# Another hand-written order for a windowed-attention and GELU-MLP kernel on one core

## Chip, cores, metric

The kernel runs on one core of a Trainium2 chip. The metric is the device time of one execution in microseconds (us). Its engines are TensorE (PE, weight loads shown as PEld), VectorE (DVE), ScalarE (ACT), GpSimd (POOL) and SyncE (SP). Each engine works through its own instructions in the order in which the program gives them; engines wait for one another, and for DMAs, on semaphores.

## What is computed

The reference is attention with a sliding window of 128 keys and 4 sink keys, followed by a two-layer MLP with a sigmoid-approximated GELU:

```python
scores = (q @ k.T) / sqrt(64)                 # q, k, v: (4 batches, 8 heads, 768, 64)
keep   = (pos_k < 4) | ((pos_q - pos_k >= 0) & (pos_q - pos_k < 128))
a      = softmax(where(keep, scores, -1e9))
x      = (a @ v) as (3072 tokens, 512)
h      = x @ w_in                             # (512, 2048)
out    = (h * sigmoid(1.702 * h)) @ w_out     # (2048, 512), float32 out
```

## The kernel before

**Tiles.** The 3072 tokens are 24 blocks of 128 (block b is row block b % 6 of batch b // 6). The first block of each batch (0, 6, 12, 18) goes first, then the others. Two blocks make a group g for the MLP.

**One block.** Its q and k come by a DMA that POOL issues and that casts them to fp16 (`qkn`, L315). They are transposed by PE (`tq`, L408, the first 8 blocks) or by a transposing DMA that SP issues (L429). PE makes the scores against the own and the previous key block (`own`, `prv`, L488; the first four blocks use L463 and a mask by matmul, L455). DVE merges the two under the window's mask (L531), takes maxima (L543, L562) and subtracts them (L600). ACT takes exp (L633; L586 for a half of the first four blocks). The result `a` is transposed, by PE for the first four blocks (`ta`, L696) and from then on by a DMA that SP issues (`at<-a`, L734). POOL cuts it into the own and the previous part by two selects (L645, L639). PE multiplies with the values (`av`, L755 for the sink keys, L761, L765), DVE normalizes (L776, L777), and PE (`tx`, L790) or a DMA transposes the result into `xT`.

**The sink keys' values.** The first four value rows of a batch come by a small SP DMA into `vsa` (L358). `vsa` is set to one beforehand by a DVE memset (L271). A product with a mask then builds `vsb` (L363), which every `av` of that batch with a previous block needs (L755).

**One group's MLP.** `hT` (L825) has 8 pieces of 32 matmuls (group 0: 16 matmuls of half the width each), ACT takes the GELU (L855), `o` (L876) has for each block four pieces of 4 matmuls with `gT`, a copy to `osb` by ACT or DVE and an SP store (L894). `w_in` and `w_out` are loaded in four quarters each by POOL (L324, L333). Piece f of `hT` needs its quarter of `w_in`; piece n of `o` needs quarter n of `w_out`.

**The order.** Nothing is scheduled by the compiler. A planner object only lists 918 operations, numbered 0 to 917 as they are added. `ORDER` (L58) is a string of tokens such as `104V`: emit operation 104 on DVE (P PE, A ACT, V DVE, G POOL, S SP). Walking through it sets the order on all five engines. `FILL` (L100) puts dummy matmuls (L905) ahead of some PE operations. `HOME` (L107) moves PSUM tiles from the ring they belong to (`mm` 3 banks, `own` 2, `pv` 2) to another one.

Operations that the change and the prediction speak of:

| number | what |
|---|---|
| 15 | DVE memset of `vsa` (L271) |
| 100 | SP load of `vsa`, batch 0 (L358) |
| 104 | building `vsb`, batch 0 (L363) |
| 49, 50 | POOL loads of q and k of block 4 (L315) |
| 35, 33 | POOL loads of `w_in`, quarters 3 and 1 (L324) |
| 38, 39, 42, 43 | POOL loads of `w_out`, quarters 0, 1, 2, 3 (L333) |
| 44, 45 | POOL loads of v, blocks 1 and 2 (L306) |
| 590, 582 | the first two pieces of `hT`, group 0 |
| 592, 593 | first two pieces of `o` of block 0; they need `w_out` quarters 0 and 1 |
| 598, 626 | first pieces of `o` of two other blocks |
| 234, 211 | SP transposes `at<-a` of blocks 2 and 1 |
| 235, 212 | POOL selects of blocks 2 and 1 |
| 236, 213 | `av` of blocks 2 and 1, first half |

POOL's loads use eight semaphores in turn, so that a load is issued only when the load eight places ahead of it has landed.

Of the kernel before, what the change touches and what calls it, by code (L numbers as in the profile page):

```python
# [55 lines left out]


ORDER = """  # L58
9V 4V 0S 17V 2V 15V 5G 13V 1S 22G 11V 19V 101S 18V 12V 7S 23G 6S 8S 28G 29G 20A 21A 3G 27G 108P 110P 109A 10V 113P
26G 16V 14V 130P 111V 114P 24G 32G 116V 131A 112A 132P 36G 133V 118A 115V 174P 37G 135P 117V 136P 175A 176P 138V  # L60
119A 154P 177V 25G 140A 120P 121A 137V 179P 31G 139V 180P 155A 152P 182V 35G 153V 141A 181V 33G 157P 184A 183V 142P
158P 34G 159V 122P 144P 185A 143A 40G 196P 123V 161V 126P 41G 145A 186P 160V 146P 198P 163A 148P 30G 127V 124P 187A
125V 46G 162A 188P 147V 164P 53G 149V 199A 166P 165V 150P 167V 189A 190P 168P 151V 128P 192P 169V 170P 129A 590P
171V 193V 582P 591A 197V 191V 172P 201P 47G 50G 586P 173A 194P 578P 583A 195V 587A 200P 579A 608P 49G 202V 610P 38G
55G 204V 203V 611A 609A 219P 221P 205V 588P 206V 589A 134A 580P 209V 208V 614P 39G 581A 105G 207V 222V 584P 42G 220V
576P 43G 585A 615A 612P 56G 577A 52G 613A 223P 604P 156A 225V 44G 226V 606P 45G 227V 616P 228V 224P 617A 607A 229V
232V 605A 230V 242P 618P 244P 231V 243V 592P 245V 626P 619A 210A 247P 246P 593P 249V 251V 248V 265P 267P 627P 250V
233A 620P 252V 266V 234S 254V 628P 268A 253V 621P 100S 255V 256A 211S 269P 622P 271V 257S 272V 594P 274V 288S 273V
629P 623P 624A 235G 270P 595P 630A 275V 104V 598P 596A 212G 599P 597S 276V 278V 631S 236P 277V 279A 238P 237V 600P
239V 59G 280S 213P 215P 51G 48G 214V 240P 601P 216V 241A 217P 602A 289P 61G 218V 290P 291V 642P 58G 292V 634P 71G  # L70
643A 294V 646P 293V 57G 295V 632P 68G 296V 647A 635A 297V 636P 62G 633A 306P 258G 640P 308V 309V 638P 641A 298V 310V
67G 73G 644P 311V 639A 637A 65G 648P 645A 654P 299A 64G 259P 655P 281G 307P 649P 312V 300S 313V 656P 314V 54G 261P
324S 315V 284P 260V 316A 650P 285V 262V 282P 657P 283V 301G 317S 178A 263P 286P 264V 651P 287V 603S 360S 664P 69G
652V 658A 662P 66G 665A 674P 60G 672P 70G 663A 675A 666P 78G 673A 325P 318G 660P 328V 327V 326P 304P 661A 667A 329V
668P 63G 330V 676P 669A 331V 74G 305V 670P 332V 302P 333V 671A 321P 303V 677P 322V 319P 682P 320V 334V 323S 342P
335A 344V 653S 345V 683P 678P 347V 343P 684P 346V 336S 348V 679P 350V 625S 351V 685P 349V 659S 352A 378P 692P 381V
686A 337G 353S 680V 379P 693A 696P 697A 380V 396S 690P 382V 80G 691A 383V 384V 688P 386V 76G 694P 385V 689A 102S
354G 387V 361P 695A 698P 364V 363V 700P 77G 699A 366V 340P 79G 701A 365V 338P 362P 388A 710P 339V 341V 355P 367V
711P 370V 368V 357P 356V 704P 389S 369V 702P 358V 371A 359S 414P 703A 705P 416V 372S 418V 712P 390G 417V 415P 706P
432S 419V 420V 713P 422V 83G 421V 707P 397P 82G 373G 708V 724P 400V 709S 399V 722P 423V 401V 714A 725A 393P 398P  # L80
402V 723A 391P 726P 392V 403V 394V 81G 716P 727A 85G 72G 718P 405V 404V 728P 719A 75G 374P 729A 717A 720P 86G 375V
106G 376P 721A 732P 406V 377V 424A 733P 395S 450P 738P 452V 407A 454V 451P 739P 453V 408S 730P 455V 456V 734P 457V
731A 715S 425S 458V 740P 433P 681S 746P 409G 436V 468S 435V 741P 747A 438V 735P 459V 742A 437V 92G 103S 758P 91G
434P 748P 759A 439V 426G 442V 736V 752P 749A 440V 756P 441V 753A 88G 744P 757A 95G 750P 745A 89G 412P 410P 413V 754P
107G 411V 429P 97G 755A 427P 430V 760P 751A 428V 443A 766P 431S 486P 767P 488V 460A 489V 444S 761P 490V 487P 762P
491V 461S 492V 768P 493V 743S 763P 494V 504S 445G 784P 764A 469P 785A 769P 472V 737S 462G 474V 495V 471V 782P 473V
772P 783A 470P 475V 87G 778P 773A 770V 98G 780P 446P 781A 84G 774P 447V 465P 775A 776P 466V 477V 779A 448P 777A 463P
476V 786P 464V 794P 449V 787A 478V 496A 467S 522P 788P 524V 525V 523P 789P 527V 479A 497S 795P 526V 528V 790P 530V
765S 529V 796P 480S 531V 532A 802P 94G 540S 498G 797P 803A 505P 798A 791P 507V 533S 96G 509V 800P 792A 481G 804P
499P 805A 810P 500V 90G 508V 814P 811A 510V 93G 501P 815A 506P 808P 511V 99G 801A 513V 484P 502V 812P 534G 482P 813A  # L90
806P 483V 809A 485V 822P 807A 514V 512V 503S 816P 515A 558P 687S 817P 793S 560V 559P 818P 562V 516S 823P 561V 563V
564V 819P 565V 567V 824P 566V 820V 568A 830P 517G 825P 831A 541P 834P 543V 826A 542P 535P 835A 827S 842P 536V 771S
544V 832P 569S 546V 833A 545V 821S 843A 547V 828P 799S 548V 836P 837A 550V 520P 829A 838P 521V 570G 549V 518P 839A
850P 551A 537P 538V 519V 844P 539S 851P 840P 552S 852P 841A 845P 573P 846P 574V 853P 553G 847P 854A 868P 855S 848A
856P 849S 869A 870P 857A 858P 871A 866P 862P 867A 859A 556P 554P 863A 557V 864P 571P 865A 860P 572V 555V 878P 861A
575S 872P 879P 873P 880P 874P 881P 886P 882V 875P 883S 887A 888P 876A 884P 877S 889A 894P 885A 890P 895A 896P 891A
892P 897A 898P 893A 906P 899A 900P 901P 907P 902P 912P 908P 903P 913P 904V 909P 914P 905S 910A 915P 911S 916A 917S
""".split()

FILL = dict(  # L100
    map(int, x.split(":"))
    for x in """
108:18 130:2 132:1 174:3 154:2 157:8 126:6 188:2 164:1 166:3
""".split()
)

HOME = dict(x.split(":") for x in "0:pv 2:mm 5:own 7:own 8:mm 9:own 10:pv 12:pv 16:own 18:mm 19:pv 21:pv 22:mm 25:own 26:pv 27:mm 28:mm 29:pv 31:pv 32:own 35:pv 37:mm 40:own 41:pv 42:mm 43:mm 44:mm 46:mm 49:pv 50:pv 51:mm 52:own 53:own 54:own 55:pv 56:own 57:pv 59:mm 61:mm 62:own 63:own 64:own 65:pv 67:own 69:own 169:own 173:own 174:own 175:pv 180:pv 181:own 183:pv 185:own 189:pv 194:pv 197:pv 199:own 200:pv".split())  # L107

# [57 lines left out]
def kernel(  # L168
# [728 lines left out]

    for n, ring in HOME.items():
        plan.bufs[int(n)].ring = ring
# [42 lines left out]
```

## Time and profile before

| | |
|---|---|
| median of 3 runs | 227.68 us (227.68 to 227.69) |
| the profiled execution, its own time | 228.61 us |
| its span in the trace | 226.9 us |
| PE busy | 218.1 us, 96% of the span |
| DVE / ACT / POOL busy | 138.7 / 127.0 / 115.3 us |
| mean granted TensorE clock | 1.0 |
| POOL's load queue (q0) | 77,024 packets, 13.37 MB |
| SP's and ACT's DMAs (q1 and q10) | 54,944 packets, 19.1 MB |

The page's "busy" of PE counts overlapping, pipelined matmuls, so that it hides short waits. What a stretch of PE costs is read from the starts of its instructions. In this execution a piece of `hT` follows the next PE operation by 0.87 us, a piece of `o` by 0.86 us, a block's scores by 0.55 us, half an `av` by 0.35 us and a group of four transposes by 0.22 us. These intervals are used for "PE work" below.

### The profile page before, as it was taken

To read this page: it belongs to the slowest core of one execution; us is meant where nothing else is said; L and a number is where in the kernel's file an instruction comes from. 1 tells how busy PE (TensorE), PEld (TensorE's weight loads), DVE (VectorE), ACT (ScalarE), POOL (GpSimd) and SP (SyncE) were. 2 spreads that over 40 slices of the span, in tenths; PEclk is the share of its full clock that TensorE was granted. 3 is DMA by queue.
4 is the path that set the end of the run, shared out by engine and by line. 5 is a ranking of instruction groups with operands and counts; after the bars stand their busy time and mean duration, and the time that the engine had idled before them with its cause. 6 is when DMAs were issued, how large, how long until landed. Compare 5 with 4: busy or idle time off the path is not lost.

```text
span 226.9 us, 5434 instructions
## 1 busy us (share of the span) xinstructions
PE 218.1 (96%) x2238; PEld 153.7 (68%) x2238; DVE 138.7 (61%) x332; ACT 127.0 (56%) x197; POOL 115.3 (51%) x127
## 2 busy tenths in 40 slices
PE   7889999999998999999999999999999999999994
PEld 4668997445774875775685685695695685775862
DVE  5799648876948288888976666668467582031001
ACT  3788675543663744767259347456656666540721
POOL 8995583029996970671980891570790321300000
PEclk9999999999999999999999999999999999999999
DMA  9999999999999999899997999998998175202202
GB/s 127 155 166 205 181 179 200 181 178 236 145 104 148 191 152 165 217 158 125 176 164 107 243 101 121 195 136 101 219 136 181 27 237 97 97 0 49 92 0 92
DMA packets 131992, 32.82 MB, mean 145 GB/s; under 512 B 124640, under 2 KB 129024, under 8 KB 131968
## 3 DMA queue, kind: packets, MB, share of 16 engines
q0 software_dynamic: 77024, 13.37, 78.1%
q1 hardware_dynamic: 53904, 18.85, 40.9%
q10 hardware_dynamic: 1040, 0.26, 0.5%
q8 instruction: 17, 0.28, 0.5%
q14 instruction: 7, 0.06, 0.1%
HBM read 27.36 MB, written 6.29 MB: 148 GB/s over the span
## 4 chain that ended last, share of the span: by engine, by line
PE 85%; DVE 7%; POOL 3%; ACT 2%; issue 1%; POOLq 0%; DVEq 0%
PE hT L825 35%; PE o L876 35%; PE own L488 3%; PE av L761 2%; PE av L765 2%; PE prv L488 2%; PE av L755 2%; DVE mx L562 2%; DVE mx L543 1%; POOL qkn L315 1%; PE tq L408 1%; DVE e L600 1%; POOL at L639 1%; ACT a L586 1%; PE tx L790 1%
## 5 line engine op out<-in xcount | busy, mean ns | idle before, releaser
L825 PE MATMUL hT<-xT,w_in 128*128 128x256 f16 (+1 forms) x832 | 91.9, 264 | 0.3 <-DVE osb L284 0.3
L876 PE MATMUL o<-w_out,gT 128*128 128x512 f16 (+1 forms) x400 | 90.5, 371 | 0.0
L855 ACT ACTIVATE gT<-hT 128x512 f16<-128x512 f32 x96 | 54.9, 597 | 49.9 <-PE hT L825 49.1
L825 PEld LDWEIGHTS <-w_in 128*128 128x128 f16 x832 | 74.0, 98 | 11.9 <-issue 0.7
L876 PEld LDWEIGHTS <-gT 128*128 128x128 f16 x400 | 36.5, 98 | 34.2 <-DVE own L531 0.4
L645 POOL TENSOR_SCALAR_AFFINE_SELECT atp<-at 128x1024 f16<-128x1024 f16 x20 | 22.1, 1104 | 71.2 <-DMA at<-a 54.7
L531 DVE COPY_PREDICATED own<-later,prv 128x512 f32<-128x512 uint16 x40 | 26.7, 692 | 25.4 <-PE prv L488 24.1
L633 ACT ACTIVATE a<-e 128x1056 f16<-128x1056 f32 (+1 forms) x24 | 23.8, 1007 | 18.2 <-issue 8.8
L543 DVE TENSOR_REDUCE mx<-own 128x4 f32<-128x512 f32 x48 | 31.9, 686 | 1.2 <-PE own L463 0.5
L600 DVE TENSOR_TENSOR e<-own,mx 128x512 f32<-128x512 f32 x44 | 28.9, 683 | 1.0
L639 POOL TENSOR_SCALAR_AFFINE_SELECT at<-at 128x1024 f16<-128x1024 f16 x20 | 22.3, 1113 | 1.4
L776 DVE RECIPROCAL rcp<-av 128x4 f32<-128x4 f32 x48 | 8.5, 176 | 23.4 <-PE av L765 23.2
L315 POOL DMA_DIRECT2D qkn<-in_k_dram x23 | 20.9, 911 | 2.8 <-DMA w_in<-in_moe_w_in_dram 2.4
L306 POOL DMA_DIRECT2D v<-in_v_dram x24 | 21.5, 907 | 0.8 <-DMA w_out<-in_moe_w_out_dram 0.8
L315 POOL DMA_DIRECT2D qkn<-in_q_dram x23 | 21.0, 913 | 1.8 <-DMA w_in<-in_moe_w_in_dram 1.7
L777 DVE TENSOR_TENSOR xn<-av,rcp 128x256 f16<-128x256 f32 x48 | 20.4, 424 | 1.7
L288 ACT COPY osb<-o 128x512 f32<-128x512 f32 (+1 forms) x17 | 9.2, 561 | 19.3 <-PE o L876 13.2
L761 PE MATMUL av<-v,at 128*128 128x65 f16 x192 | 16.7, 194 | 0.5 <-POOL at L639 0.4
L284 DVE COPY osb<-o 128x512 f32<-128x512 f32 x8 | 5.5, 688 | 18.5 <-PE o L876 18.1
L761 PEld LDWEIGHTS <-at 128*128 128x128 f16 x192 | 14.0, 98 | 3.1 <-POOL at L639 1.3
L765 PE MATMUL av<-v,atp 128*128 128x65 f16 x160 | 14.9, 194 | 0.0
L488 PEld LDWEIGHTS <-qkT 64*128 64x128 f16 x320 | 9.4, 94 | 7.0 <-issue 5.7
(59 smaller groups left out, 176.9 us busy)
## 6 DMA issues: line engine op xcount, KB each, us to landing
out_dram<-osb SPq DMA_DIRECT2D x23, 256.0 KB, 2.6
v<-in_v_dram POOLq DMA_DIRECT2D x24, 128.0 KB, 5.4
qkn<-in_q_dram POOLq DMA_DIRECT2D x23, 128.0 KB, 5.1
qkn<-in_k_dram POOLq DMA_DIRECT2D x23, 128.0 KB, 5.1
w_in<-in_moe_w_in_dram POOLq DMA_DIRECT2D x4, 512.0 KB, 10.1
w_out<-in_moe_w_out_dram POOLq DMA_DIRECT2D x4, 512.0 KB, 10.2
at<-a SPq DMA_TRANSPOSE x20, 3.5
rawk<-in_k_dram ACTq DMA_DIRECT2D x1, 256.0 KB, 4.5
```

Source lines behind the costliest of these rows:

```text
L306: return sw(key, 0.88, lambda: nc.gpsimd.dma_start(v65[:, b, :, 0:D], src), 1.0, deps=[z_1] + deps, after=after)
L315: key, 0.88, lambda: nc.gpsimd.dma_start(buf()[:, i, w], src), 0.9,
L531: nc.vector.copy_predicated(out=own[l](), mask=later.unsqueeze(1).to_broadcast((P, 4, P)), data=prv[l]())
L543: lambda l=l, own=own, small=small, r=r: nc.vector.tensor_reduce(out=small[:, l], in_=own[l](), axis=AX.X, op=ALU.max, negate=r == 0),
L600: nc.vector.tensor_tensor(out=e32()[:, 512 * l : 512 * l + 512].rearrange("p (j s) -> p j s", j=4), in0=own[l](), in1=small[:, l].unsqueez ...
L633: nc.scalar.activation(out=a16()[:, lo:hi], in_=e32()[:, lo:hi], func=AF.Exp, scale=factor)
L639: nc.gpsimd.affine_select(out=dst()[:, lo : lo + n], in_=at()[:, lo : lo + n], pattern=[[0, n], [1, P]], compare_op=ALU.is_ge, fill=0.0, b ...
L645: nc.gpsimd.affine_select(out=dst()[:, lo : lo + n], in_=at()[:, lo : lo + n], pattern=[[0, n], [-1, P]], compare_op=ALU.is_gt, fill=0.0, ...
L761: nc.tensor.matmul(av()[:, j], ato()[:, c], v65[:, b, h], start=(r == 0), stop=(r == 0))
L825: nc.tensor.matmul(ht()[:, n], w_in16[:, c, bass.ts(f, P)], xt[g]()[:, tok, c], start=(c == 0), stop=(c == 3))
L855: lambda fs=fs, cols=cols, gt=gt, ht=ht: nc.scalar.activation(out=gt()[:, fs[0] : fs[-1] + 1, cols], in_=ht(), func=AF.Gelu_apprx_sigmoid),
L876: nc.tensor.matmul(po(), gt()[:, F, bass.ts(t, P)], w_out16[:, F, cols], start=(F == 0), stop=(F == NF - 1))
```

## The change

The tokens of `ORDER` are the same 918 operations in another sequence on all engines. 29 operations run on another engine: 28 copies or evictions and sink-key copies swap between ACT and DVE (14 each way), and the building of `vsb` for batch 0 (104) goes from DVE to POOL. `FILL` has 43 dummy matmuls where it had 46. `HOME` gives other banks to tiles of the first eight blocks and the first four MLP groups. ACT switches between its exp and its GELU table 22 times where it did so 20 times. Of the loads that POOL issues, the first 22 move the same number of bytes in both orders, and so do the loads up to and including number 45. The diff, cut to lines that the prediction speaks of (long lines are shown whole):

```diff
 ORDER = """
-125V 46G 162A 188P 147V 164P 53G 149V 199A 166P 165V 150P 167V 189A 190P 168P 151V 128P 192P 169V 170P 129A 590P
-171V 193V 582P 591A 197V 191V 172P 201P 47G 50G 586P 173A 194P 578P 583A 195V 587A 200P 579A 608P 49G 202V 610P 38G
-55G 204V 203V 611A 609A 219P 221P 205V 588P 206V 589A 134A 580P 209V 208V 614P 39G 581A 105G 207V 222V 584P 42G 220V
-576P 43G 585A 615A 612P 56G 577A 52G 613A 223P 604P 156A 225V 44G 226V 606P 45G 227V 616P 228V 224P 617A 607A 229V
-233A 620P 252V 266V 234S 254V 628P 268A 253V 621P 100S 255V 256A 211S 269P 622P 271V 257S 272V 594P 274V 288S 273V
-629P 623P 624A 235G 270P 595P 630A 275V 104V 598P 596A 212G 599P 597S 276V 278V 631S 236P 277V 279A 238P 237V 600P
...
+47G 30G 127V 150P 164P 189A 151V 166P 128P 197V 190P 192P 129V 49G 590P 165A 199A 193V 167A 191V 582P 591A 112V 194P
+168P 170P 201P 169V 586P 50G 15V 195A 171V 100S 578P 583A 587A 172P 200P 579A 173V 219P 202V 616P 220A 203V 608P
+104G 617A 205V 588P 38G 609A 204V 221P 206V 42G 589A 580P 209V 208V 222A 39G 614P 207V 55G 156V 224P 223P 615A 612P
+581A 226V 43G 225V 610P 613A 227V 53G 52G 228V 229V 576P 230V 231V 232V 56G 244P 577A 606P 245A 618P 607A 611A 604P
+619A 605A 584P 242P 592P 243V 585A 265P 44G 45G 246P 266A 267P 249V 233A 598P 251V 247P 626P 248V 250V 593P 210A
+252V 234S 254V 599P 255V 134A 253V 627P 600P 211S 268A 256A 594P 270P 257S 269P 628P 595P 271V 272V 274V 288S 601P
+235G 273V 596V 620P 602A 275V 629P 276V 212G 277V 621P 630A 278V 279A 236P 631S 238P 237V 622P 239V 280S 213P 65G
...
-108:18 130:2 132:1 174:3 154:2 157:8 126:6 188:2 164:1 166:3
+108:19 176:3 120:3 179:1 142:2 157:1 186:12 198:2
...
```

In the order before, 15V stands among the first tokens and 101S (the `vsa` load of batch 1) is SP's third DMA; in the new order 101S comes after 280S.

## The prediction

> **What bounds the kernel now.** I read the page first, then PE's waits, then the timelines of PE, POOL and SP around the longest waits, then the DMA queues in short windows.
>
> ```profile
> PE 218.1 (96%) x2238; PEld 153.7 (68%) x2238; DVE 138.7 (61%) x332; ACT 127.0 (56%) x197; POOL 115.3 (51%) x127
> ```
>
> PE is the bound nearly everywhere. From its first L825 at 20.8 us to the end, its starts follow each other at the fixed intervals given above, but for about 6.4 us: some 2 us in gaps of 0.1, 0.93 us at block 2's and block 1's `av`, and about 3.4 us in single waits, most of them later. The same matmuls run in both orders, so a new order can win only from the 20.8 us ahead of the first L825 and from these 6.4 us; it can lose whatever new waits cost. The 0.93 us is the most telling wait (timelines of PE and POOL):
>
> ```profile
> 51.95 0.27 PE L755 MATMUL av<-vsb,at 128*128 128x260 f16 x1
> 52.35 0.20 PE L761 MATMUL av<-v,at 128*128 128x65 f16 x1
> ...
> 54.56 0.20 PE L761 MATMUL av<-v,at 128*128 128x65 f16 x1 [0.38 <-POOL at L639]
> ```
> ```profile
> 20.03 0.87 POOL L315 DMA_DIRECT2D qkn<-in_k_dram  x1 [0.80 <-DMA w_in<-in_moe_w_in_dram]
> 22.54 0.87 POOL L315 DMA_DIRECT2D qkn<-in_k_dram  x1 [1.64 <-DMA w_in<-in_moe_w_in_dram]
> 25.08 0.87 POOL L315 DMA_DIRECT2D qkn<-in_q_dram  x1 [1.67 <-DMA w_in<-in_moe_w_in_dram]
> 25.94 0.76 POOL L333 DMA_DIRECT2D w_out<-in_moe_w_out_dram  x1
> ...
> 36.16 0.88 POOL L306 DMA_DIRECT2D v<-in_v_dram  x1 [0.80 <-DMA w_out<-in_moe_w_out_dram]
> 49.62 1.09 POOL L645 TENSOR_SCALAR_AFFINE_SELECT atp<-at 128x1024 f16<-128x1024 f16 x1 [12.59 <-DMA at<-a]
> ```
>
> PE waits for POOL's selects, and POOL had idled 12.59 us for a transposing DMA. That DMA was issued at 42.04, but POOL's load queue q0 was still full. In the DMA view of 42 to 45 us, with two transposes and the `vsa` load issued, only q0 moves data:
>
> ```profile
> q0 software_dynamic: 2920, 0.48, 212.1%
> q8 instruction: 1, 0.02, 2.0%
> issues: line engine op xcount, KB each, median us to landing
> at<-a SPq DMA_TRANSPOSE x2, 6.1
> vsa<-in_v_dram SPq DMA_DIRECT2D x1, 8.0 KB
> ```
>
> The last load of that run (v, issued at 36.16) lands 12.8 us later, at 49.0; POOL starts 0.65 us after that. So here the end of POOL's first 32 loads sets the time.
>
> **The start.** Up to the first maximum (DVE L543 at 7.96) the new order has the same chain: `qkn`'s cast of k on ACT to 5.92, the transposes, two copies one behind the other, the scores at 7.52. The cast of q goes to DVE; it has until 5.92 before anyone waits. From 7.96 DVE's new queue up to the copy that releases the first L825 is 12 operations on a whole score tile (0.69 the first, 0.72 two that need the one before, 0.61 apart the other nine), 3 copies (0.34), 4 normalizations (0.55), a memset (0.1) and that copy (0.41): 11.4 us, hence 19.3. Two places wait for a copy on ACT, 0.4 to 0.9 us together: first L825 at 19.8 to 20.3 instead of 20.82. Two half `av`s (0.24 us) move behind it, so the gain is 0.3 to 0.8 us; PE reaches the first L876 (592) at about 37.2 (before 37.80). But block 2's `av` can't start before the loads have drained, so this gain ends as a longer wait there: I count it 0.
>
> **The moved `vsb`: the main term.** Removed: 0.68 us of DVE; added: 1.16 us of POOL.
>
> ```profile
> L363 POOL TENSOR_TENSOR vsb<-vsa,ownm x3: 1147/1164/1191, 30.1 to 134.7; 32x520 f16<-32x520 f32 x3
> L363 DVE TENSOR_TENSOR vsb<-vsa,ownm x1: 681/681/681, 50.7 to 50.7; 32x520 f16<-32x520 f32 x1
> ```
>
> What counts is its place. On POOL, 104 stands between load 50 and `w_out`'s quarter 0, and it waits for DMA 100, which waits for memset 15. DVE now does 15 behind the first normalization of block 12, whose `av` stands behind the two first L825 pieces: 20.1 + 1.8 + 0.2, then 0.3 + 0.6 for `av` and normalization, gives 23.0; SP issues 100 at 23.2. Queued behind 104 on POOL: all four quarters of `w_out`, q and k of blocks 4, 5 and 7, v of blocks 1 and 2, both selects.
>
> When does 100 land? From below: small SP loads at 2.4 to 3.9 us, with q0 just starting, took 3.9 us:
>
> ```profile
> later<-clater SPq DMA_DIRECT2D x1, 32.0 KB, 3.9
> ```
>
> That gives 27.1. From above: it comes behind all loads issued before it. Load 22 was issued at 22.54 in the profile before and landed 9.9 us later, at 32.5; the same bytes stand ahead of it in the new order. I take the upper end, 32.2, since 42 to 45 us is the nearest row (a full q0, the same small load). The other way round, q0 got almost nothing behind SP's transposes between 98.6 and 99.9 us, though a load issued at 95.89 landed only at 102.7:
>
> ```profile
> q1 hardware_dynamic: 1171, 0.30, 122.3%
> q0 software_dynamic: 50, 0.01, 6.9%
> ```
>
> So what was issued first goes first. The Trainium skill says otherwise (DMA: Bandwidth & Descriptors, "Queues, rings and completion order"): each DMA engine takes turns between its queues, a packet of descriptors at a time. The two windows disagree with that; by it DMA 100 would land near the lower end and this term would be 0.
>
> With 32.2, 104 ends at 33.4, and quarter 0 of `w_out` is issued at 33.4 with q0 empty, instead of joining a full queue. From an idle queue a load of 128 KB took 3.3 us (issue at 64.56) to 5.1 us (54.45). Successive landings were 2.5 us apart for 512 KB and 0.85 for 128 KB, so 1.65 more: 5.0 to 6.75. It lands at 38.4 to 40.2, while a full queue would give 32.5 + 2.5 = 35.0. All later loads shift by 3.4 to 5.2 us; I take 4.3, landing at 39.3.
>
> On PE: 592 waits 39.3 − 37.2 = 2.1 us. 593 needs quarter 1, now third in the queue: + 5.1 us, against 3.7 us of PE work between the two (592, 598, 626, scores, transposes): another 1.4. Then 10.1 us of work to block 2's `av`: 54.6. Its select can start only when the loads have drained, 49.0 + 4.3, + 0.65: 53.95, and its second matmul comes 2.7 us behind that as before: 56.65 against 52.35. Block 1's `av` follows in the same way. Both orders have done the same PE work by then (but for three dummy matmuls, 0.33 us, which the wait swallows), so the whole remainder is 4.3 us late.
>
> **The rest.** Two waits behind DVE between 56 and 72 us may shorten, since DVE catches up while PE waits:
>
> ```profile
> PE av L755 <- DVE e L600: 0.6, 1, 0.6
> PE own L488 <- DVE e L600: 0.4, 1, 0.4
> ```
>
> Against that, POOL now issues 11 loads instead of 9 before block 3's select (0.88 us each), and block 4's `av` comes 2.2 us of PE work sooner after its scores with a margin of 1.15 before: up to 1.0 lost. Bounds −1.0 to +1.0, taken −0.4. The two more table loads (1.28 us each) lie on ACT, which is 56% busy and waits 49 us for L825; if they came just ahead of a needed GELU they would cost 1.3 each. Copies between DVE and ACT: 0.69 against 0.56 us, even numbers both ways, covered by the same idle time. From 76 us on, PE lost about 3 us over 150 us in the old order; I take the same. The tail still ends with a half-width eviction on ACT (0.37) and its store: 0.
>
> Sum: 0 + 4.3 − 0.4 = +3.9 us. On the profiled execution's 228.61 that is 232.5; on the median, 0.93 us lower for the same kernel, 231.6.
>
> **Rivals.** (1) *Faster or level: the small load is not held up.* Then 104 ends by about 28.3. It decides at 29.0: q0's last packets ahead of it move until about 31.0, and a load's first packets come 2.0 us after its issue. POOL delays nothing, block 2's `av` starts as before, and the two DVE waits may go: 227.68 − 0.7 = 227.0, between 226.2 and 228.4. For it: the 3.9 us of the early small loads. Against it: 42 to 45 us. The Trainium skill's rule on turns, above, would bring about this case. (2) *Half held up*: 100 lands at 29 to 31, the queue runs empty for 1 to 3 us: 228.5 to 230. (3) *The late loads cost twice*: the selects of blocks 3 and 4 come late too, since POOL's 11 loads start 4.3 us later and PE runs closer behind: the +1.0 instead of −0.4, and as much again at block 5: about 234.
>
> **Chances.** Forecast 0.56; (1) 0.27, of which 0.17 faster by over 0.2% (0.46 us, about what a measurement of this kernel can tell from no change), 0.04 within, 0.06 slower; (2) 0.10; (3) 0.07. Faster 0.17, same 0.04, slower 0.79. The forecast's own range is 230.1 (3.4 − 1.0 = +2.4) to 233.3 (5.2 + 0.4). To leave out no more than 2 in 10, the range reaches through (2) into (1): 227.0 to 233.3.
>
> **What would show it.** Right: POOL's timeline has L363 ending near 33 with some 9 us of idle time ahead of it, released by DMA `vsa`; the first `w_out` issue at 33 to 34; q0 nearly empty around 32 to 35; PE idle ahead of the first L876, released by DMA `w_out`, and again some 5 us later; block 2's `av` near 56.6. Wrong: L363 on POOL before 29, q0 full through 35, and block 2's `av` at 52; then the sign hangs on the waits of 56 to 76 us alone. A first L825 later than 20.8 would show the start misjudged.

## The result, and the profile after

The new order takes 230.87 us (median of 6 executions, 229.37 to 233.20), the old one 227.69 beside it; the ratio is 1.010, with a 95% interval of 1.006 to 1.014. A second comparison on another occasion gave 231.06 us (9 executions, 229.20 to 233.65) and 1.012 (1.008 to 1.016). The kernel is slower by 2.3 to 3.2 us, as forecast; how it gets there is not quite what was forecast. Ratios in this document leave out disturbed executions; medians are over all of them.

The profiled execution of the new order took 232.85 us (span 231.1). Its first row has the same work on PE:

```profile
PE 219.5 (95%) x2235; PEld 154.3 (67%) x2235; DVE 137.1 (59%) x334; ACT 130.7 (57%) x196; POOL 116.1 (50%) x128
```

The group of `vsb` (minimum, median and maximum in ns, first and last start) is now POOL's alone:

```profile
L363 POOL TENSOR_TENSOR vsb<-vsa,ownm x4: 1119/1164/1204, 29.3 to 139.6; 32x520 f16<-32x520 f32 x4
```

POOL's timeline (start, duration, engine, line, operation; in brackets the idle time before it and what ended it) shows the wait that the prediction is about:

```profile
29.28 1.12 POOL L363 TENSOR_TENSOR vsb<-vsa,ownm 32x520 f16<-32x520 f32 x1 [5.86 <-DMA vsa<-in_v_dram]
30.36 2.30 POOL L333 DMA_DIRECT2D w_out<-in_moe_w_out_dram  x3
...
39.43 0.88 POOL L306 DMA_DIRECT2D v<-in_v_dram  x1 [1.63 <-DMA w_out<-in_moe_w_out_dram]
50.49 1.09 POOL L645 TENSOR_SCALAR_AFFINE_SELECT atp<-at 128x1024 f16<-128x1024 f16 x1 [10.18 <-DMA at<-a]
```

POOL stood still for 5.86 us ahead of `w_out` and issued quarter 0 at 30.36 instead of 25.94. SP had issued the load of `vsa` at 23.56. The DMA view of the stretch that follows, 30.5 to 33 us, shows the hole in the load queue (packets, MB, and the time that the packets took, as a share of the 16 DMA engines' time); the second fence is the same stretch of a kernel without the wait (`e1_vsa_early`, below):

```profile
q0 software_dynamic: 421, 0.11, 49.1%
```
```profile
q0 software_dynamic: 822, 0.50, 139.6%
```

0.11 MB instead of 0.50 at 0.2 MB/us are 1.9 us of lost transfer. But PE hardly waits for `w_out`: its first L876 (592) starts at 37.51, 0.29 us sooner than before, with quarter 0 landed at 36.46; 593 starts at 41.77, where quarter 1 landed at 41.73, and at the pace of the matmuls before it (0.22 apart, the last at 41.27) it would have been 41.49: 0.3 us. PE's timeline shows the price elsewhere, 15 us later:

```profile
52.01 0.27 PE L755 MATMUL av<-vsb,at 128*128 128x260 f16 x1
56.09 0.22 PE L761 MATMUL av<-v,at 128*128 128x65 f16 x1 [3.80 <-DMA v<-in_v_dram]
...
57.16 1.90 PE L876 MATMUL o<-w_out,gT 128*128 128x512 f16 x4
```

PE waits 3.80 us for the values of block 2 themselves. This load (45, the last of the 32) landed at 56.04; before it landed at 48.97. In the kernel without the wait it landed at 49.18. So 1.9 us of hole have become 7 us at the end of the queue. Where the other 5 come from is visible in the DMA view of 47 to 49 us:

```profile
q1 hardware_dynamic: 805, 0.21, 80.5%
q0 software_dynamic: 814, 0.10, 79.3%
```

SP's transposes (q1) and POOL's loads (q0) move almost the same number of packets, though the two transposes were issued at 41.80 and 44.07, after all the loads. From 42 to 45 us, as in the profile before, q0 had still been alone:

```profile
q0 software_dynamic: 929, 0.54, 132.5%
```

A last cost is in the last line of the PE fence: four matmuls that took 1.02 us elsewhere took 1.90. The windows of the same profile (stretch, length, busy time of PE, PEld, DVE, ACT, POOL, granted clock, DMA share, GB/s) show why:

```profile
50.00:53.00 3.00, 2.28 (x12) 0.98 (x10) 1.86 (x6) 1.83 (x3) 2.18 (x2) 1.00 1.79 165
53.00:57.00 4.00, 0.91 (x15) 0.84 (x15) 0.24 (x2) 0.04 (x1) 1.82 (x2) 0.75 1.30 148
57.00:60.00 3.00, 3.00 (x26) 1.77 (x24) 1.20 (x5) 0.00 (x0) 3.00 (x5) 0.50 1.00 227
60.00:63.00 3.00, 3.00 (x37) 1.85 (x35) 1.75 (x5) 0.71 (x2) 3.00 (x4) 0.69 2.19 156
```

After the idle time PE's granted clock is 0.50 throughout 57 to 60 us; 0.75 and 0.69 in the stretches beside it put the half speed at 55.0 to 61.9 us. In another profiled execution (229.66 us, `c0_after`) the same wait was 3.13 us and the clock stayed at 1.00; executions with a mean clock of 1.0 took 229.2 to 229.9, two at 0.998 took 230.4 and 231.2, those at 0.985 to 0.993 took 230.6 to 233.7.

These two profiles of one kernel show what the half speed costs. At block 2's `av` the slower one is 0.65 us behind (56.09 against 55.44, the landing of v). At the transposes of 62.08 (58.91 in `c0_after`) it is 3.17 us behind, and at the end 3.19 (232.85 against 229.66). So 2.5 of the 3.2 us between them are lost between these two places, where the clock is at 0.5.

The Trainium skill (TensorE: Matmul & The Clock Gate, "What's actually happening") says that the clock halves after an idle window of about 3.4 us, and that the window isn't tied to the kernel; 3.80 with and 3.13 without a drop agree with that. A third wait doesn't: in `e9_vsa_28us` (below) PE waited only 2.54 us, up to 45.95, and its clock was 0.50 from 46 to 49 us. So the length of a wait alone doesn't tell whether the clock falls.

### The profile page after: what moved, and what is told of

It reads as the page before. It is cut to its first block, busy times and chain, and to the rows that moved or that the text cites. A ratio compares the mean times of both kernels' runs of the same rounds, so it can differ in the third digit from the quotient of the medians.

```text
span 231.1 us, 5425 instructions
## 1 busy us (share of the span) xinstructions
PE 219.5 (95%) x2235; PEld 154.3 (67%) x2235; DVE 137.1 (59%) x334; ACT 130.7 (57%) x196; POOL 116.1 (50%) x128
## 3 DMA queue, kind: packets, MB, share of 16 engines
q10 hardware_dynamic: 1040, 0.26, 0.5%
## 4 chain that ended last, share of the span: by engine, by line
PE 72%; DMA 15%; DVE 9%; issue 1%; ACT 1%; POOL 1%; POOLq 0%; DVEq 0%
PE hT L825 31%; PE o L876 29%; DMA v<-in_v_dram 7%; DMA w_out<-in_moe_w_out_dram 3%; DVE mx L543 3%; PE av L761 3%; DMA vsa<-in_v_dram 2%; PE own L488 2%; PE av L765 2%; DVE e L600 2%; PE av L755 2%; DMA rawq<-in_q_dram 2%; PE prv L488 2%; DVE own L531 1%; PE tx L790 1%
## 5 line engine op out<-in xcount | busy, mean ns | idle before, releaser
L825 PE MATMUL hT<-xT,w_in 128*128 128x256 f16 (+1 forms) x832 | 92.6, 264 | 0.0
L876 PE MATMUL o<-w_out,gT 128*128 128x512 f16 (+1 forms) x400 | 91.9, 375 | 0.1
L825 PEld LDWEIGHTS <-w_in 128*128 128x128 f16 x832 | 73.9, 98 | 11.7
L876 PEld LDWEIGHTS <-gT 128*128 128x128 f16 x400 | 37.1, 98 | 35.6 <-issue 1.5
L639 POOL TENSOR_SCALAR_AFFINE_SELECT at<-at 128x1024 f16<-128x1024 f16 x20 | 21.8, 1091 | 1.4
L761 PE MATMUL av<-v,at 128*128 128x65 f16 x192 | 17.5, 198 | 3.9 <-DMA v<-in_v_dram 3.8
L284 DVE COPY osb<-o 128x512 f32<-128x512 f32 (+1 forms) x8 | 5.2, 653 | 19.8 <-PE o L876 19.8
L761 PEld LDWEIGHTS <-at 128*128 128x128 f16 x192 | 14.7, 100 | 2.5 <-POOL at L639 0.9
L765 PE MATMUL av<-v,atp 128*128 128x65 f16 x160 | 15.8, 199 | 0.0
L765 PEld LDWEIGHTS <-atp 128*128 128x128 f16 x160 | 12.0, 101 | 3.9 <-issue 3.2
```

The source lines that it names most:

```text
L761: nc.tensor.matmul(av()[:, j], ato()[:, c], v65[:, b, h], start=(r == 0), stop=(r == 0))
L765: nc.tensor.matmul(av()[:, j], atp()[:, c], v65[:, b - 1, h], start=False, stop=(j == 3))
L825: nc.tensor.matmul(ht()[:, n], w_in16[:, c, bass.ts(f, P)], xt[g]()[:, tok, c], start=(c == 0), stop=(c == 3))
L876: nc.tensor.matmul(po(), gt()[:, F, bass.ts(t, P)], w_out16[:, F, cols], start=(F == 0), stop=(F == NF - 1))
```

## The experiments

Theory A: POOL's wait for `vsa`, ahead of loads that it has still to issue, is the cost. Theory B: it is the place of the last loads in their queue. Theory C: it is something else in the new order. Each kernel below is the new order with one edit, except `e2`, which is the old order with one. The diffs are cut: a line shows only the tokens around the place that changes.

**The wait taken away: vsa early.** Memset 15 and load 100 go back to the start, as in the old order; 104 stays on POOL at its new place.

```diff
-9V 4V 18V 16V 5G 17V 2V 13V 19V
+9V 4V 18V 16V 5G 17V 2V 15V 13V 19V
-25G 8S 7S 136P
+25G 8S 7S 100S 136P
-586P 50G 15V 195A 171V 100S 578P
+586P 50G 195A 171V 578P
```

> The new order, but the memset of vsa (15) is among DVE's first operations and the small load 100 stands behind SP's fifth DMA, so that it lands before 16 us and POOL's 104 waits for nothing. Theory A (the wait of POOL for vsa empties the load queue, and every later load is late): 104 ends at about 24.5, w_out quarter 0 is issued at about 26 instead of 30.4, quarter 1 lands 2 to 2.5 us sooner than 41.7, v of blocks 1 and 2 land at 49 to 51 instead of 54.5 and 56.0, the 3.8 us wait of block 2's av is gone, and the time is 227.0 to 228.2. Theory B (v of blocks 1 and 2 stand behind one more load of q and k than before and share the DMA engines with SP's transposes; the vsa wait adds little): v of block 2 lands at 53 or later, PE still waits 2 us or more, 229 to 230. Theory C (neither: the other swaps of engines, banks and order cost the time): as the new order, about 230, and PE loses its time elsewhere.

227.28 us (226.78 to 228.24, 12 executions); ratio to the old order 0.9956 (0.9934 to 0.9978). POOL and PE:

```profile
23.26 1.15 POOL L363 TENSOR_TENSOR vsb<-vsa,ownm 32x520 f16<-32x520 f32 x1
24.34 0.81 POOL L333 DMA_DIRECT2D w_out<-in_moe_w_out_dram  x1
```
```profile
51.88 0.27 PE L755 MATMUL av<-vsb,at 128*128 128x260 f16 x1
51.99 0.19 PE L761 MATMUL av<-v,at 128*128 128x65 f16 x1
```

Theory A. Both waits are gone (PE keeps one of 0.40 us for POOL's selects at block 1's `av`), load 45 lands at 49.18, and everything else of the change, taken together, makes the kernel 0.7 us faster. So the wait alone costs 231.06 − 227.28 = 3.8 us between medians. Part of that is the fallen clock of some executions: between the two profiled ones, both at a granted clock of 1.0, it is 229.66 − 227.35 = 2.3 us.

**The control.**

> The new order itself, beside the others on the same chip. All theories: 229.4 to 230.9; POOL waits 5 to 6 us for vsa ahead of w_out quarter 0 and PE waits 2 to 4 us for v at block 2's av. If that second wait is much shorter in another execution while the time stays, theory B and the profile's main wait are in doubt.

231.06 us, as said above: POOL waited 5.70 us, PE 3.13, load 45 landed at 55.39.

**The same move in the old order.**

```diff
-9V 4V 0S 17V 2V 15V 5G
+9V 4V 0S 17V 2V 5G
-47G 50G 586P 173A
+47G 50G 15V 586P 100S 173A
-610P 38G
+610P 104G 38G
-253V 621P 100S 255V
+253V 621P 255V
-275V 104V 598P
+275V 598P
```

> The order before, with only the place of the three vsa operations of the new one: memset 15 behind the issue of load 50, load 100 behind it on SP, 104 on POOL ahead of w_out quarter 0. Theory A: POOL waits about 6 us for vsa, quarter 0 is issued at about 30 instead of 25.9, the loads of v of blocks 1 and 2 land 2 to 4 us later than 47.6 and 49.0, block 2's and block 1's av wait 0.5 to 2 us more, 228.2 to 229.7. The prediction's own step (all of the 4.3 us): 232. Theory B: the loads' order is the old one, the queue catches up, 227.5 to 227.9. Theory C: 227.7, no difference.

In this kernel the late memset also overwrites the sink values of batch 1, which were loaded at the start, so that these values are missing from its output; the work is the same. 229.23 us (228.59 to 229.73), ratio 1.0041 (1.0018 to 1.0064). POOL waits only 2.82 us, since the old order issues load 49 at 25.20, between 50 and 104. `w_out` quarter 0 lands 0.85 us later than before and load 45 2.8 us later, at 51.79; PE's wait at block 2's and block 1's `av` is 1.6 us, for POOL's selects. Theory A in kind and size, with half the wait; C can't explain it.

**The last loads in another order.**

```diff
-226V 43G 225V
+226V 43G 44G 45G 225V
-265P 44G 45G 246P
+265P 246P
```

> The new order with the wait of 104 left as it is; only loads 44 and 45 (v of blocks 1 and 2) are moved ahead of 53, 52 and 56 (q and k of later blocks), right behind w_out quarter 3. Theory A: quarters 0 and 1 of w_out are as late as in the new order and PE is 1.5 us late at 593, but the av of block 2 is late only through its transposes: 228.5 to 229.3. Theory B: v of blocks 1 and 2 land at 48 to 50 instead of 54.5 and 56.0, the 3.8 us wait is gone, the loads of q and k are late by 1 to 3 us and nobody waits for them before 62 us: 227.0 to 228.3. Theory C: about 230, as the new order.

235.91 us (231.85 to 239.93), ratio 1.021 (1.015 to 1.026): slower still, and every theory had it faster or level. The loads of v landed at 50.19 and 52.62, but now 53, 52 and 56 (q and k of later blocks) came last, at 53.50, 54.57 and 56.95, and somebody did wait for them:

```profile
57.25 0.20 PE L761 MATMUL av<-v,at 128*128 128x65 f16 x1 [2.03 <-POOL at L639]
66.02 0.29 PE L488 MATMUL own<-qkT 64*128 64x128 f16 x2 [6.68 <-DMA qkT<-qkn]
```

SP could issue the transpose of these q and k (L429) only at 57.11, against 53.40 in the new order; it then took 8.9 us instead of 4.8, with POOL's next loads issued from 57.14 on, and the scores that need it (289) stood at 66.02 instead of 62.40. I had read the 62 us at which PE needs the scores as the time by which the loads are needed, and left out the transpose between. The last load of the queue is late in either order; here changing places only chose who waits.

**Only POOL's place, or only the engine.** First 104 moved behind the last load, still on POOL; then 104 on DVE; then DVE and the early load together.

```diff
-608P 104G 617A 205V 588P 38G
+608P 617A 205V 588P 38G
-265P 44G 45G 246P
+265P 44G 45G 104G 246P
```

> The new order with memset 15 and load 100 as late as they are there; only POOL's place for the building of vsb (104) is moved, from ahead of w_out quarter 0 to behind the last of the 32 loads (45). Theory A (what costs is that POOL waits ahead of loads that it has still to issue): w_out quarter 0 is issued at about 24, v of block 2 lands at about 49, no wait of PE at block 2's av, 227.0 to 227.6, as with the early vsa. Theory A' (what costs is the late small load itself, or 1.1 us of work on POOL): little is gained, 229 to 231.

```diff
-608P 104G 617A 205V 588P 38G
+608P 617A 205V 588P 38G
-252V 234S 254V
+252V 104V 234S 254V
```

> The new order with load 100 as late as it is there, but 104 (vsb) given back to DVE, ahead of the transpose 234. Theory A (POOL's wait): as with 104 behind the loads on POOL or with the early vsa, 227.0 to 228.1, w_out quarter 0 issued at 23.3 to 24.3. If 1.1 us of POOL's work ahead of the loads mattered by itself, this would be the fastest of the three. If the small load at 28 us itself delays the later loads, it stays at 227.8 as with 104 last on POOL.

> The new order with both: memset 15 and load 100 early, and 104 on DVE. Theory A: no further gain over the early vsa alone, 226.9 to 227.6, since POOL has 1.1 us to spare ahead of a full queue. If POOL's 1.1 us mattered: 226.2 to 226.8.

227.81 us for the place (ratio 0.9996, 0.9976 to 1.0017), 227.63 for the engine (0.9983, 0.9962 to 1.0004), 227.36 for engine and early load (0.9978, 0.9956 to 1.0000). Each of the three takes 3.2 to 3.7 us back, so neither the late load, nor POOL's 1.1 us of work, nor the engine is the cost by itself: it is the wait in front of the loads. The 0.3 to 0.5 us by which the two kernels with the late small load are behind the early one are hardly more than the intervals, and stay open. In their profiles load 45 landed at 51.73 (the place) and 50.57 (the engine), later than the 49.18 of the early vsa, and PE still waited 1.1 and 0.9 us for POOL's selects at the `av`s of blocks 2 and 1.

**How much wait.** Memset and load sooner than in the new order (the load issued at 21.35 instead of 23.6 to 23.7), and later (27.75).

```diff
-192P 129V 49G
+192P 129V 15V 100S 49G
-586P 50G 15V 195A 171V 100S 578P
+586P 50G 195A 171V 578P
```

> The new order with memset 15 and load 100 some 2.7 us sooner: load 100 is issued at about 21.0. With the 4.4 us that a first packet took behind a full load queue it lands at 26.5; POOL then waits 3 us instead of 5.8 and issues w_out quarter 0 at about 27.7. Theory of the threshold (the prediction's rival 1: as long as 104 ends before 29.0 the queue doesn't run empty and nothing is lost): 227.0 to 227.7. Theory of the straight line (each us of POOL's wait costs about 0.65 us, 3.8 over 5.8): 229.2. Theory that q0's loads go first in the order of issue: load 100 lands at 30 or later and the time stays at 230 to 231.

```diff
-586P 50G 15V 195A 171V 100S 578P
+586P 50G 195A 171V 578P
-608P 104G 617A 205V 588P 38G
+608P 617A 205V 15V 100S 588P 104G 38G
```

> The new order with memset 15 and load 100 some 4.2 us later: load 100 is issued at about 27.9 and lands at about 32.3, the value that the prediction had assumed. Prediction's own steps: 104 ends at 33.4, w_out quarter 0 lands at 38.4 to 40.2, PE waits 1 to 3 us ahead of its first L876, 231.6 on the scale of the prediction. Theory A with sharing (loads that are still open when SP's transposes start at 45.5 us move at a third of their rate): every load is 3 us later again than in the new order before that, v of block 2 lands at 60 or later, PE waits 2 us at w_out and 6 us or more at v, 234 to 238.

228.14 us (ratio 1.0004, 0.9977 to 1.0031) and 235.40 us (1.036, 1.031 to 1.040). POOL of the first and the second:

```profile
27.72 1.12 POOL L363 TENSOR_TENSOR vsb<-vsa,ownm 32x520 f16<-32x520 f32 x1 [4.28 <-DMA vsa<-in_v_dram]
28.79 2.30 POOL L333 DMA_DIRECT2D w_out<-in_moe_w_out_dram  x3
```
```profile
32.41 1.12 POOL L363 TENSOR_TENSOR vsb<-vsa,ownm 32x520 f16<-32x520 f32 x1 [8.85 <-DVE own L531]
33.48 2.30 POOL L333 DMA_DIRECT2D w_out<-in_moe_w_out_dram  x3
```

(The second wait was put down to a DVE operation that had long ended; it is the load, issued at 27.75.) PE of the second:

```profile
39.26 1.04 PE L876 MATMUL o<-w_out,gT 128*128 128x512 f16 x4 [1.62 <-DMA w_out<-in_moe_w_out_dram]
...
45.95 6.09 PE L876 MATMUL o<-w_out,gT 128*128 128x512 f16 x20 [2.54 <-DMA w_out<-in_moe_w_out_dram]
...
59.59 0.19 PE L761 MATMUL av<-v,at 128*128 128x65 f16 x1 [1.52 <-DMA v<-in_v_dram]
```

In the second row the first two pieces took 3.3 us (45.95 to 49.28) instead of 1.7, at a clock of 0.50. PE waited for v behind it, which landed only at 59.55, so that this slower stretch didn't move the `av`.

| kernel | POOL's wait, us | `w_out` quarter 0 issued | load 45 landed | median, us |
|---|---|---|---|---|
| vsa early | 0 | 24.34 | 49.18 | 227.28 |
| issue at 21.35 | 4.28 | 28.79 | 51.77 | 228.14 |
| new order (`c0_after`) | 5.70 | 30.29 | 55.39 | 231.06 |
| issue at 27.75 | 8.85 | 33.48 | 59.55 | 235.40 |

The first 4.5 us of delay cost 0.9 us, the next 1.5 us cost 2.9, the next 3.2 us cost 4.3. So the line isn't straight: the price of a further us rises from 0.2 to between 1.4 and 1.9. But it isn't nothing at the start either. Where it bends is less sure, since the median of the new order holds executions with a fallen clock: between the profiled executions (227.35, 228.42, 229.66 and 234.90 us) the three steps cost 1.1, 1.2 and 5.2, or 0.2, 0.8 and 1.6 for each us.

**Whose fault the end of the queue is.** SP is held up instead, by a spare memset and load (into `hold`, a spare tile) behind 272V, and the transposes 234, 211 and 257 come after it; POOL's wait stays.

```diff
-252V 234S 254V 599P 255V 134A 253V 627P 600P 211S 268A 256A 594P 270P 257S 269P 628P 595P 271V 272V 274V
+252V 254V 599P 255V 134A 253V 627P 600P 268A 256A 594P 270P 269P 628P 595P 271V 272V x 234S 211S 257S 274V
...
+            if item == "x": nc.vector.memset(hold[:, :], 1.0); nc.sync.dma_start(hold[:, :], vin[0, :, 0:4, :]); continue
```

> The new order with POOL's wait for vsa left in; SP is held up instead: a DVE memset and a load of 8 KB into a spare tile are put ahead of the transposes of a for blocks 2 and 1 (234, 211), at about 48.5 us, so that these transposes are issued some 6.5 us later, when the load queue has almost drained. Theory of sharing (the last five loads are late because SP's transposes take two thirds of the DMA engines' time from 46 us on): load 45 (v of block 2) lands at 50.3 to 52 instead of 55.4, though POOL waits as long as before; PE no longer waits for v but for the transposes and selects, and the time is 229.5 to 232. Theory that the late start alone makes the loads late: load 45 lands at 54 to 55.5 as before, and the time is 231 to 235.

230.41 us (230.00 to 231.66; ratio 1.011, 1.007 to 1.015). SP's and POOL's timelines, and the load queue of 47 to 49 us:

```profile
49.57 4.25 SPq L734 DMA_TRANSPOSE at<-a  x3
```
```profile
52.97 1.09 POOL L645 TENSOR_SCALAR_AFFINE_SELECT atp<-at 128x1024 f16<-128x1024 f16 x1 [12.32 <-DMA at<-a]
```
```profile
q0 software_dynamic: 2451, 0.31, 242.9%
```

Without transposes beside it the load queue moved 2,451 packets in those 2 us, three times the 814 of the new order. Load 45 landed at 51.05 instead of 55.39 (`c0_after`) or 56.04, though POOL had waited as long. The transpose of block 2, issued 7.8 us later than in the new order, landed 3.4 us after its issue, at 52.97, and the select started 2.5 us later than in the profile above and 1.4 us later than in `c0_after`. Theory of sharing. (By bytes the transposes had two thirds of what moved from 47 to 49 us in the new order, 0.21 MB of 0.31; by time, which the expectation speaks of, it was half, 80.5 against 79.3%.) PE now waits for POOL's selects (2.04 us), so the time moves little.

**Whether the clock is the spread.** 28 dummy matmuls ahead of block 2's `av` (236), in `FILL`.

```diff
-108:19 176:3 120:3 179:1 142:2 157:1 186:12 198:2
+108:19 176:3 120:3 179:1 142:2 157:1 186:12 198:2 236:28
```

> The new order with 28 more dummy matmuls (0.11 us each, 3.1 us) ahead of block 2's first av half, where PE waits 3 to 4 us for v. Theory of the clock (where the new order takes 231 to 233 us instead of 229.5, PE's granted clock fell behind that idle time): PE stays busy through the wait, the mean clock stays at 0.997 or above in every execution, and all times lie between 229.2 and 230.3. Theory of the transfers (the spread is that of the landing of v): the spread stays 229 to 233, or the dummies come on top.

231.90 us (230.40 to 232.31; ratio 1.017, 1.013 to 1.020). The mean clock was 0.998 to 1.000 in all six executions, and still none was under 230.4. With the clock kept, the ratio is no better than the control's 1.008 to 1.016. So a fallen clock isn't needed for a long execution, and the spread of 1.9 us that is left here has no shown cause. But this doesn't clear the clock in the new order itself: of the 3.2 us between its two profiles, 2.5 are lost while the clock is at 0.5, and only 0.65 by the landing of v. What the dummies cost over all six executions wasn't separated; in the profiled one block 2's first product with v started at 55.48 us, against 55.44 in `c0_after`, so that there they only filled the wait.

## Why the prediction was right, and where its steps were not

The forecast of 231.6 us stands beside 230.87, and its mechanism holds: moved `vsb`, POOL's wait ahead of the loads, late loads, a longer wait at block 2's `av`. Three of its steps were off, the first two in directions that cancelled, so that the closeness of the number is in part luck. Executions with a mean clock of 1.0 took 229.2 to 229.9, which lies in the price that the prediction gave to its rival 2 (228.5 to 230); the fallen clock, which lifts the median, had no term in the sum.

- **The landing of load 100: forecast 32.2, measured 29.2 to 29.3.** The step took "what was issued first goes first" from two windows of the profile. It isn't so. POOL's load 50, issued at 22.55, needed 10.0 us behind the full queue; the small load, issued a microsecond later, needed 5.7 (4.4 of them to its first packet). With q0 empty, first packets of SP came 0.83 to 1.18 us after the issue, with the long queues of 21 to 28 and 42 to 46 us 3.3 to 4.7 us, and 2.6 us in `e9`, where that queue was nearly through; from then on the two share. The window of 42 to 45 us, on which I relied, showed that delay and not an order: in the old order the first packet of the transpose issued at 42.04 moved at 45.3, with loads still on their way. The other window, 98.6 to 99.9, reads the same way the other way round: from 96 to 99.3 us q0 moved 1,040 packets, as many as one load of 128 KB has, and then none until 100.0, 4.1 us after the issue of the next load at 95.89. The Trainium skill's rule of turns (DMA: Bandwidth & Descriptors, "Queues, rings and completion order") fits the windows from 46 us on, 814 and 805 packets, and not these first microseconds. Landing at 29.2 to 29.3 is rival 2, "half held up", which I had priced at 228.5 to 230.
- **The price of a hole: forecast 4.3 us for 104 ending at 33.4; measured 8.1.** That is `e9` against the early vsa: it makes just that case (104 ends 33.5) and bears out the next two steps: `w_out` quarter 0 lands at 39.22 (forecast 39.3), 592 waits 1.62 (2.1). 593 waits 2.54 (1.4), since quarter 1 lands at 45.91 and not at 44.4. But the working shifted all later loads by the same amount. In fact the shift grows down the queue: in the control, against the early vsa, from 1.2 us at quarter 0 over 2.8 at quarter 3 to 6.2 at load 45, because whatever is still open when SP's transposes start moving, at 45.3 to 46.4 us, goes on at a third of its rate (407 packets per us against 1,226). In `e10`, where the transposes start only when the queue is nearly empty, the shift doesn't grow: 3.0 at quarter 3 (46.31) and 1.9 at load 45 (51.05). 1.9 us of hole became 3.8 us of time between medians, 2.3 between profiles at full clock.
- **Where PE waits.** The forecast had 2.1 us at the first L876 and 1.4 at the second; measured 0 and 0.3. The wait at block 2's `av` came as forecast (56.09 against 56.65), but for v itself and not for POOL's select. The step had tied that select to the end of the loads; it began at 50.49, 5.5 us before the last one landed.
- **The decisive point at 29.0** (rival 1) is roughly right: with 104 ended at 28.8 the kernel lost 0.9 us against the early vsa, at 30.3 it lost 3.8 by medians and 2.3 by profiles. The prediction had this loss at nothing before the point.
- **Rival 3**, late loads that cost twice, didn't come. In `c0_after` PE is 3.45 us behind `e1` at block 2's `av`, 3.09 at block 1's and 2.4 at the end: later waits give some of it back.

The start came out nearly as worked out: first L825 at 20.29 to 20.44 (forecast 19.8 to 20.3, before 20.82), and in the new order this gain is swallowed by the wait for v. Without that wait it isn't: in `e1` block 2's second `av` half starts at 52.23 against 52.69. Start and rest together, forecast 0 − 0.4 us, measured −0.7 with the wait removed (0.9956 of 228.0 is −1.0); which later wait gave the rest wasn't tested.

## What to carry to other kernels

An engine that issues loads should wait for as little as it can, however short the instruction that waits: ask of each instruction on POOL what is queued behind it, and move it behind the loads, to another engine, or its input ahead. Look at when the next user of the DMA engines starts: loads still open then went on at a third of their rate here, so that a hole early in the queue was paid at its end. Swapping loads within the late queue only chose who waits, and the reader of a load may be a transpose that nobody counted. Before a difference between two executions is put down to a wait, compare the granted clock behind it: here the half speed cost more than the longer wait.

## What the hardware showed

- POOL's loads (128-byte packets) ran at 1,226 packets per us alone, 2,451 in 47 to 49 us, and at 407 beside SP's transposes; the transposes moved 0.21 MB in those 2 us and 0.42 in 2 us alone (`e10`, 51 to 53). Together they moved 0.31 MB in 2 us, no more than the loads alone and less than the transposes alone.
- A transpose issued at 49.57 into a drained queue landed sooner after its issue (3.4 us, by the start of POOL's select) than one issued at 41.80 into a full one (8.7 us).
- A PE wait of 3.80 us was followed by a granted clock of 0.5 (0.50 from 57 to 60 us, 0.69 from 60 to 63); one of 3.13 us was not, but one of 2.54 us was (`e9`: 0.50 from 46 to 49 us).
